# Softmax sums of the first tile: two pairs through VectorE transposes instead of TensorE, with another order of work in front of the first matmuls

## The chip, the cores and the metric

The kernel runs on one core of one Trainium2 chip. The metric is device time in microseconds, from the program's start to its end. Before the change it is 294.37 us, the median of three runs (294.26 to 294.83); the profiled execution has a span of 293.0 us. Times inside the text are microseconds from the start of that span unless they are called durations.

## The reference

Two stages are computed one after the other. The first is attention within chunks of 64 rows, for 8 batches and 8 heads of 64; the second is a feed-forward block with an exact GELU on the 4608 tokens that come out.

```python
# attention: q, k, v are [8, 8, 576, 64]; chunks of 64 rows
scores = (1/8) * q_c @ k_c.T                      # 64 x 64 per chunk and head
attn = exp(scores - max) ; attn = attn / sum(attn)
x = (attn @ v_c)  ->  [4608, 512]                 # heads side by side
# feed-forward
h = x @ w_in                                      # [4608, 2048]
g = 0.5 * h * (1 + erf(h / sqrt(2)))
out = g @ w_out                                   # [4608, 512], fp32
```

The kernel leaves the maximum out (the scores are small) and divides by the sum at the end: it multiplies `attn @ v` by the reciprocal of the sum of the exponentials.

## The kernel before

The tokens are taken in nine tiles of 512 (`MT`), numbered t = 0 to 8. Heads are taken as four pairs g = 0 to 3 (`G`), so that a pair fills 128 partitions. For every tile the attention gives `x`, [128, 4, 512]: one pair per K slice of the first matmul. Then mm1 makes 16 blocks of `h` (four matmuls of 128x512 each, one per K slice) and mm2 makes the output from them. While TensorE runs mm1 and mm2 of tile t, the attention of tile t+1 is fitted in between. Only tile 0 has nothing to hide behind: its attention, and the casts of the first weights, run before the first matmul of mm1.

The program gives the order of instructions itself: on each engine they run in the order in which the program issues them.

The attention of tile 0, one pair at a time, is: `T` (transposes of q and k on TensorE, and copies from PSUM), `S` (scores on TensorE, exp on ScalarE into `pT`), the sum, and `A` (attn @ v on TensorE, times the reciprocal on VectorE).

```python
    def att_Tk(t, g, copies):                       # k of a pair: two halves, two copies
        tp = transposed(t, "k", g)
        for r in range(2):
            sl = slice(CH * r, CH * (r + 1))
            copies[r](k_bds[g][sl, :, sl]..., tp[sl])

    def att_sum(t, g, later=False):                 # sums by VectorE
        pT = tiles[t]["pT", g]
        sum_ps = ps_at.tile([P, MT], f32, tag="at", name="sum_ps")
        nc.tensor.matmul(sum_ps[:], ones_bd[:], pT[:], start=True, stop=True)
        ...
        nc.vector.transpose(t1[:], sum_ps[:].rearrange("p (n e) -> p n e", e=32))
        def rest_of_it():
            nc.vector.reciprocal(r1[:], t1[:, :, 0])
            nc.vector.transpose(rc[:], r1[:].to_broadcast([P, NB, 32]))
        ...

    def att_sum_pe(t, g):                           # sums and their spreading by TensorE
        pT = tiles[t]["pT", g]
        sT = ps_at.tile([P, MT // P, 2], f32, tag="at", name="sT")
        for m in range(MT // P):
            nc.tensor.matmul(sT[:, m], pT[...][:, m * P:(m + 1) * P], ones_r[:], start=True, stop=True)
        rr = work.tile([P, MT // P, 2], f32, tag="rr", name="rr", bufs=2)
        nc.vector.reciprocal(rr[:], sT[:])

        def spread():
            pool, tag = (ps_mm, "mm") if g < 2 else (ps_tp, "tp")
            rc_ps = pool.tile([P, NB, 32], f32, tag=tag, name="rc_ps")
            flat = rc_ps[:].rearrange("p n e -> p (n e)")
            for m in range(MT // P):
                for r in (1, 0):
                    nc.tensor.transpose(flat[0:CH * (r + 1), m * P:(m + 1) * P],
                                        rr[:, m, r:r + 1].to_broadcast([P, CH * (r + 1)]), ident_f[:])
            rc = work.tile([P, NB, 32], f32, tag="rc", name="rc", bufs=4)
            nc.scalar.copy(rc[:], rc_ps[:])
            tiles[t]["rc", g] = rc
        return spread

    def att_av(t, g):
        av_ps = ps_at.tile(...)
        for i in range(CT):
            nc.tensor.matmul(av_ps[:, i, :], v_bds[t % NV][:, i, g, :], st["pT", g][:, i, :], ...)
        nc.vector.tensor_tensor(x, av, rc, op=mybir.AluOpType.mult)
    ...
    def mm1_slot(t, f, n=1, between={}):            # tile 0 begins with n = 2: f0 and f1 slice by slice
        for ks in range(KS):
            for a in range(n):
                nc.tensor.matmul(h_ps[a][:], w_in_sb[:, ks, (f + a) * P:...], st["x"][:, ks, :], ...)
```

The start of the program, in its order (cut from the scores of pair 0 on):

```python
        S_[0]()
        T[3]()
        cast_qk(0, "q", 2, DV)
        keep_warm(1)
        T[4]()
        keep_warm(1)
        S_[1]()
        cast_qk(0, "q", 3, DV)
        p0 = att_sum_pe(0, 0)
        T[5]()
        p0()
        T[6]()
        T[7]()
        p1 = att_sum_pe(0, 1)
        S_[2]()
        p1()
        keep_warm(1)
        S_[3]()
        p2 = att_sum_pe(0, 2)
        p2()
        A[0]()
        A[1]()
        p3 = att_sum_pe(0, 3)
        p3()
        A[2]()
        A[3]()
        win.append(load_w_in(NWC - 1))
        wout = [load_w_out(0)]
        act_table(Act.Gelu)
        for i, eng in enumerate((PO, DV, DV, PO)):
            win[0](i, eng)                          # casts of w_in block f = i
        ... # then the casts of the other w_in chunks, by DV and PO in turn,
            # with two memsets of v_bd on PO between them
        phase(0, ...)                               # mm1 and mm2 of tile 0
```

`DV`, `AC` and `PO` are a copy or cast on VectorE, ScalarE and GpSimd. `keep_warm(n)` runs n matmuls on zeros, whose result nobody reads. `w_in` comes in four chunks of four blocks: chunks 0 and 1 in two DMAs each (blocks 0-1 and 2-3), chunks 2 and 3 in one.

Of the kernel before, what the change touches and what calls it, by code (L numbers as in the profile page):

```python
# [11 lines left out]
def kernel(  # L12
# [9 lines left out]
    nc = tc.nc  # L22
    P = 128
    f32 = mybir.dt.float32
# [4 lines left out]
    CH = 64  # L29
    NC = S // CH  # L30
    J = 4
# [115 lines left out]
    def att_Tq(t, g, copy):  # L147
        tp = transposed(t, "q", g)
        qT = work.tile([P, CT, CH], bf16, tag="qT", name="qT", bufs=5)
        copy(qT[:].rearrange("p i (c j) -> p i c j", j=J), tp)  # L150
        tiles[t]["qT", g] = qT

    def att_Tk(t, g, copies):
        tp = transposed(t, "k", g)
        for r in range(2):
            sl = slice(CH * r, CH * (r + 1))
            copies[r](k_bds[g][sl, :, sl].rearrange("p i (c j) -> p i c j", j=J), tp[sl])  # L157


    def flip(t, nm):  # L160
# [101 lines left out]
    def att_sum_pe(t, g):  # L262
# [4 lines that stand above are left out]
            nc.tensor.matmul(sT[:, m], pT[:].rearrange("p i c -> p (i c)")[:, m * P:(m + 1) * P], ones_r[:],  # L267
                             start=True, stop=True)
        rr = work.tile([P, MT // P, 2], f32, tag="rr", name="rr", bufs=2)
        nc.vector.reciprocal(rr[:], sT[:])  # L270

        def spread():


            pool, tag = (ps_mm, "mm") if g < 2 else (ps_tp, "tp")
            rc_ps = pool.tile([P, NB, 32], f32, tag=tag, name="rc_ps")
            flat = rc_ps[:].rearrange("p n e -> p (n e)")
            for m in range(MT // P):
                for r in (1, 0):
                    nc.tensor.transpose(flat[0:CH * (r + 1), m * P:(m + 1) * P],  # L280
                                        rr[:, m, r:r + 1].to_broadcast([P, CH * (r + 1)]), ident_f[:])
            rc = work.tile([P, NB, 32], f32, tag="rc", name="rc", bufs=4)
            nc.scalar.copy(rc[:], rc_ps[:])
            tiles[t]["rc", g] = rc
        return spread

# [17 lines left out]
    def att_units(t, cq=DV, ck=DV):  # L304
        tiles[t]["x"] = xpool.tile([P, G, MT], bf16, tag="x", name="x")
        T = []
        for g in range(G):
            T += [lambda g=g: att_Tq(t, g, cq), lambda g=g: att_Tk(t, g, (AC, DV) if t == 0 and g > 1 else [AC if t == 0 or g < 2 else DV] * 2)]
        S_ = [lambda g=g: att_S(t, g) for g in range(G)]
        if t > 1:  # L310
            T = [lambda g=g: flip_k(t, g, ck) for g in range(G)]
            S_ = [lambda g=g: (att_S_flipped(t, g), att_part(t, g)) for g in range(G)]
        if t > 0:
            U = [lambda g=g: att_total(t, g, g + 2) for g in (0, 2)] + [lambda g=g: att_rc(t, g) for g in range(G)]
        else:
            U = [lambda g=g: att_sum(t, g) for g in range(G)]
        A = [lambda g=g: att_av(t, g) for g in range(G)]
        return T, S_, U, A
# [111 lines left out]
    def load_w_out(c):  # L430
        raw = stage_tile()[:].rearrange("p (f n) -> p f n", f=FC)
        nc.sync.dma_start(raw, w_out_v[:, c * FC:(c + 1) * FC, :])

        def cast(i, copy):
            copy(w_out_sb[:, c * FC + i, :], raw[:, i, :])
        return cast
# [13 lines left out]
    def act_table(func):  # L450
        nc.scalar.activation(act_scratch[:], rest[:, 0:1], func)  # L451

    with tc.manual_schedule():
        for g in range(G):
            for nm in "qk":
                load_qk(0, nm, 2 * g, 2 * g + 2)
        load_v(0)
        win = [load_w_in(c, 2 if c < 2 else 1) for c in range(NWC - 1)]
        act_table(Act.Exp)
        keep_warm(7)  # L460
        zero_k(k_bds[0], nc.gpsimd)
        zero_k(k_bds[1], nc.gpsimd)
        zero_v(0, nc.vector)
        T, S_, U, A = att_units(0, DV, AC)
        cast_qk(0, "k", 0, PO)
        zero_k(k_bds[2], nc.gpsimd)
        cast_qk(0, "k", 1, PO)
        zero_k(k_bds[3], nc.gpsimd)
        cast_qk(0, "k", 2, PO)
        cast_qk(0, "k", 3, PO)  # L470
        for g in range(G):
            cast_v(0, 0, PO, slice(g, g + 1))
            cast_v(0, 1, PO, slice(g, g + 1))
        cast_qk(0, "q", 0, DV)
        T[0]()
        cast_qk(0, "q", 1, DV)
        T[1]()
        keep_warm(3)
        T[2]()
# [5 lines that stand above are left out]
        keep_warm(1)  # L485
        S_[1]()
        cast_qk(0, "q", 3, DV)
        p0 = att_sum_pe(0, 0)
        T[5]()
        p0()  # L490
        T[6]()
        T[7]()
        p1 = att_sum_pe(0, 1)
        S_[2]()
        p1()
        keep_warm(1)
        S_[3]()
        p2 = att_sum_pe(0, 2)
        p2()
        A[0]()  # L500
        A[1]()
        p3 = att_sum_pe(0, 3)
        p3()
        A[2]()
        A[3]()
        win.append(load_w_in(NWC - 1))
        wout = [load_w_out(0)]
        act_table(Act.Gelu)
        for i, eng in enumerate((PO, DV, DV, PO)):
            win[0](i, eng)  # L510
        load_qk(1, "q")
        wout.append(load_w_out(1))
        for c in range(1, NWC):
            for i in range(4):
                win[c](i, DV if i % 2 == 0 else PO)
            if c == 1:
                load_qk(1, "k")
            else:
                wout.append(load_w_out(c))
            if c < 3:  # L520
                r = slice(CH * (c - 1), CH * c)
                o = slice(CH * (2 - c), CH * (3 - c))
                nc.gpsimd.memset(v_bds[1][r, :, :, o], 0.0)
        for i in range(FC):
            wout[0](i, DV if i % 2 == 0 else PO)
        load_v(1)
        for g in range(G):
            cast_qk(1, "q", g, DV if g == 0 else PO)
        for i in range(FC):
            wout[1](i, DV if i % 2 == 0 else PO)  # L530
        for g in range(G):
            cast_qk(1, "k", g, DV if g % 2 == 0 else PO)
        for i in range(FC):
            wout[2](i, PO)
        for i in range(2):
            wout[3](i, PO)
        for g in range(G):
            for r in range(2):
                cast_v(1, r, PO, slice(g, g + 1))

        T, S_, U, A = att_units(1, AC, AC)
        def next_qk():
            for nm in "qk":
                load_qk(2, nm)
        over = []

        def sums():
            over.append(att_sums(1))
            over[0](1)
        phase(0, {}, {0: [lambda: act_table(Act.Exp)],  # L550
                      2: [T[0]], 3: [T[2]], 4: [T[4], T[6]], 7: [T[1], T[3]], 8: [T[5], S_[0]],
                      9: [T[7], S_[1], next_qk], 10: [S_[2], lambda: att_sum(1, 0), lambda: wout[3](2, DV)],
                      11: [lambda: wout[3](3, AC), S_[3]], 12: [sums],
                      13: [A[0], lambda: over[0](2), lambda: over[0](3), U[3]], 14: [A[1], U[4]], 15: [A[2], U[5]]},
              by_rows=True)
        last_av = {1: [A[3], lambda: rows_out(0, 3)]}
        pool_cast_qk(2)
        for t in range(1, NT):
            nxt = t + 1 < NT
            if nxt:  # L560
                T, S_, U, A = att_units(t + 1)
                for nm in "qk":
                    flip(t + 1, nm)
                if t == 1:
                    load_v(2)
                for r in range(2):
                    cast_v(t + 1, r, PO)
                if t + 2 < NT:
                    load_all(t + 2)
                    pool_cast_qk(t + 2)  # L570
            e1, e2 = {}, {}
            if nxt:
                e1 = {8: [T[0]], 10: [T[1]], 12: [T[2]], 14: [T[3]]}
                e2 = {0: [lambda: act_table(Act.Exp), S_[0]], 1: [S_[1]], 2: [S_[2]],
                      3: [S_[3], U[0]], 5: [U[1], lambda: act_table(Act.Gelu)],
                      7: [U[2], A[0]], 8: [U[3], A[1]], 10: [U[4], A[2]], 12: [U[5], A[3]]}
            phase(t, e1, e2, between=last_av if t == 1 else {})
# [28 lines left out]
```

The softmax here doesn't subtract the row's maximum and nothing guards it: scores larger than these inputs give would overflow.

## Time and profile before

| engine | busy us | share of the span |
|---|---|---|
| PE (TensorE matmul) | 281.5 | 96% |
| DVE (VectorE) | 155.0 | 53% |
| ACT (ScalarE) | 169.5 | 58% |
| POOL (GpSimd) | 98.7 | 34% |

The profile is one execution, recorded by the hardware. TensorE is busy nearly throughout, so the places where it is not are what is looked at; they lie in the first 22 us. A view of busy time by stretches gives TensorE 3.33 us of the 5 from 10 to 15, 3.51 of the 5 from 15 to 20, and 3.66 of the 5 from 20 to 25; from 57 to 100 it is busy all 43. The granted clock is 1.00 in every stretch. The share of the DMA engines is 1.06 of their capacity, as the view counts it, from 15 to 30, so data is arriving as fast as it can while the attention of tile 0 is worked out.

In a line of the timeline the columns are: start, duration, engine, line of the kernel, operation, tile written `<-` tiles read, shape, count, and in brackets how long the engine had been idle before and what ended that. In the chain of waits a line is a piece of the chain that ended last: start, duration, and what it was.

### The profile page before, as it was taken

Reading aid. Unit: us, or ns where it says so; the run is one execution under the profiler, and the core shown is the slowest. Engines: PE = TensorE matmul, PEld = TensorE weight load, DVE = VectorE, ACT = ScalarE, POOL = GpSimd, SP = SyncE. Lnnn points to the kernel's source line nnn. Section 1 sums busy time; section 2 is a strip of 40 time slices with the busy share of each in tenths; the row PEclk is TensorE's granted clock in tenths of the full one; section 3 lists DMA queues with packets and bytes.
Section 4 is the critical chain, followed back from the end, with each engine's and each line's share of the span. In section 5 each row is a group of like instructions: output and inputs, shape, how many; then the busy total and the mean of one; then the engine's idle time right before and its main releaser. Section 6 shows DMA issues by size and latency. Waiting matters only on the chain.

```text
span 293.0 us, 4901 instructions
## 1 busy us (share of the span) xinstructions
PE 281.5 (96%) x1874; PEld 140.6 (48%) x1874; DVE 155.0 (53%) x264; ACT 169.5 (58%) x328; POOL 98.7 (34%) x136
## 2 busy tenths in 40 slices
PE   7669999999999999999999999999999999999994
PEld 2554455445544554455445444554455445544443
DVE  5649317744842794449525964496168515850011
ACT  3546756978536853685268627862786268726400
POOL 6759758605650850075005600650003520000000
PEclk9999999999999999999999999999999999999999
DMA  6899998899859913991399339922999990020032
GB/s 213 218 359 404 396 340 230 276 217 284 215 185 296 247 73 97 283 267 64 99 217 298 95 100 275 267 69 103 192 127 125 235 186 2 36 106 4 0 72 72
DMA packets 96887, 53.79 MB, mean 184 GB/s; under 512 B 68576, under 2 KB 89312, under 8 KB 96864
## 3 DMA queue, kind: packets, MB, share of 16 engines
q1 hardware_dynamic: 96704, 53.36, 68.8%
q8 instruction: 14, 0.23, 0.3%
q10 hardware_dynamic: 160, 0.13, 0.2%
q14 instruction: 9, 0.07, 0.1%
HBM read 36.70 MB, written 9.44 MB: 157 GB/s over the span
## 4 chain that ended last, share of the span: by engine, by line
PE 90%; DVE 3%; DMA 2%; ACT 1%; SPq 1%; issue 1%; DVEq 0%
PE h_ps L331 42%; PE y_ps L347 37%; PE y_ps L387 3%; PE av_ps L292 2%; DMA arrival<-in_q_dram 2%; PE s_ps L180 2%; PE rc_ps L280 1%; DVE x L299 1%; PE y_ps L372 1%; SPq L112 1%; DVE rc L259 1%; PE tp L144 1%; ACT k_bd L157 1%; PE s_ps L192 0%; ACT rb L229 0%
## 5 line engine op out<-in xcount | busy, mean ns | idle before, releaser
L331 PE MATMUL h_ps<-x,w_in_sb 128*128 128x512 bf16 x576 | 126.3, 379 | 1.5 <-DVE w_in_sb L427 1.3
L334 ACT ACTIVATE h<-h_ps 128x512 bf16<-128x512 f32 x144 | 85.5, 597 | 63.6 <-PE h_ps L331 63.5
L347 PE MATMUL y_ps<-w_out_sb,h 128*128 128x512 bf16 x512 | 120.5, 379 | 0.0
L331 PEld LDWEIGHTS <-w_in_sb 128*128 128x128 bf16 x576 | 56.2, 98 | 69.3 <-DVE w_in_sb L427 1.6
L347 PEld LDWEIGHTS <-h 128*128 128x128 bf16 x512 | 46.0, 98 | 46.5 <-issue 0.2
L172 DVE COPY k_bd<-k_t 64x512 bf16<-64x512 bf16 x56 | 35.2, 629 | 50.4 <-DMA k_t<-k_nat 49.4
L133 POOL CAST q_nat<-arrival 128x512 bf16<-128x512 f32 x31 | 20.9, 711 | 96.2 <-DMA arrival<-in_q_dram 96.2
L137 POOL CAST v_bd<-arrival 64x512 bf16<-64x512 f32 (+1 forms) x30 | 36.4, 1212 | 20.1 <-DMA arrival<-in_v_dram 13.1
L299 DVE TENSOR_TENSOR x<-av_ps,rc 128x512 bf16<-128x512 f32 x36 | 24.7, 691 | 6.5 <-PE av_ps L292 2.9
L133 POOL CAST k_nat<-arrival 128x512 bf16<-128x512 f32 x34 | 20.1, 626 | 13.6 <-DMA arrival<-in_k_dram 13.5
L239 DVE STREAM_TRANSPOSE pt<-pT 128x256 f32<-128x256 f32 x28 | 12.2, 437 | 22.9 <-ACT pT L183 22.9
L451 ACT ACT_TABLE_LOAD x18 | 23.1, 1283 | 1.1 <-PEq L590 0.7
L356 DVE COPY y_sb<-y_ps 128x512 f32<-128x512 f32 x11 | 7.6, 689 | 29.2 <-PE y_ps L347 29.2
L356 ACT COPY y_sb<-y_ps 128x512 f32<-128x512 f32 x24 | 13.8, 580 | 14.7 <-PE y_ps L347 14.4
L259 DVE STREAM_TRANSPOSE rc<-rb 128x512 f32<-128x512 f32 x31 | 21.4, 692 | 0.2 <-ACT rb L229 0.2
L242 DVE TENSOR_REDUCE part<-pt 128x16 f32<-128x512 bf16 x28 | 19.2, 686 | 1.0
L250 ACT COPY other<-part 32x32 f32<-32x32 f32 x56 | 12.1, 215 | 10.4 <-DVE part L242 9.9
L292 PEld LDWEIGHTS <-v_bd 128*128 128x128 bf16 x288 | 13.0, 98 | 7.6
L183 ACT ACTIVATE pT<-s_ps 128x512 bf16<-128x512 f32 x28 | 14.7, 590 | 0.0
L292 PE MATMUL av_ps<-pT,v_bd 128*128 128x64 bf16 x288 | 13.9, 193 | 0.0
L180 PEld LDWEIGHTS <-k_bd 128*128 128x128 bf16 x224 | 10.4, 98 | 6.6
L387 PE MATMUL y_ps<-w_out_sb,h 128*128 128x512 bf16 x48 | 12.0, 379 | 0.3 <-ACT h L334 0.3
(67 smaller groups left out, 141.2 us busy)
## 6 DMA issues: line engine op xcount, KB each, us to landing
arrival<-in_v_dram SPq DMA_DIRECT2D x72, 128.0 KB, 4.1
out_dram<-y_sb SPq DMA_DIRECT2D x32, 256.0 KB, 2.1
arrival<-in_q_dram SPq DMA_DIRECT2D x7, 1024.0 KB, 6.2
arrival<-in_k_dram SPq DMA_DIRECT2D x7, 1024.0 KB, 9.1
arrival<-in_moe_w_out_dram SPq DMA_DIRECT2D x4, 1024.0 KB, 12.5
arrival<-in_moe_w_in_dram SPq DMA_DIRECT2D x4, 512.0 KB, 6.0
arrival<-in_moe_w_in_dram SPq DMA_DIRECT2D x2, 1024.0 KB, 9.5
arrival<-in_q_dram SPq DMA_DIRECT2D x4, 256.0 KB, 5.4
```

Of the source, the lines that this page charges most:

```text
L133: copy(st[nm][:, g].rearrange("p j r d -> p r j d"), st[nm + "f"][:, 2 * g:2 * g + 2])
L137: copy(v_bds[t % NV][sl, :, gs, sl].rearrange("p i g d -> p g i d"), tiles[t]["vf"][sl, gs])
L172: copy(k_bds[g][sl, :, sl].rearrange("p i (c j) -> p i c j", j=J), src[sl])
L259: nc.vector.transpose(rc[:], src.to_broadcast([P, NB, 32]))
L292: nc.tensor.matmul(av_ps[:, i, :], v_bds[t % NV][:, i, g, :], st["pT", g][:, i, :], start=True, stop=True)
L299: nc.vector.tensor_tensor(x, av, rc, op=mybir.AluOpType.mult)
L331: nc.tensor.matmul(h_ps[a][:], w_in_sb[:, ks, (f + a) * P:(f + a + 1) * P], st["x"][:, ks, :], start=(ks == 0), stop=(ks == KS - 1))
L334: nc.scalar.activation(st["h"][:, f + a, :], h_ps[a][:], Act.Gelu)
L347: nc.tensor.matmul(y_ps[:], st["h"][:, f, ms * P:(ms + 1) * P], w_out_sb[:, f, :], start=(f == 0), stop=(f == FF - 1))
L356: (AC if ms < 3 and t + 1 < NT else DV)(y_sb[:], y_ps[:])
L387: nc.tensor.matmul(tiles[t]["y_ps", ms][:], tiles[t]["h"][:, f, ms * P:(ms + 1) * P], w_out_sb[:, f, :], start=(f == 0), stop=False)
L451: nc.scalar.activation(act_scratch[:], rest[:, 0:1], func)
```

## The change

The sums of pairs 0 and 1 of tile 0 go from the TensorE form (`att_sum_pe`) back to the VectorE form (`att_sum`); pairs 2 and 3 keep the TensorE form, whose spreading now always uses the `ps_mm` buffers. Both halves of every k copy of tile 0 are ScalarE's (VectorE had one half of pairs 2 and 3). The sums of pairs 2 and 3 are both made ahead of the first attn @ v, and the spreadings go between A[0], A[1] and A[2]. Two `keep_warm(1)` are added. One of the two VectorE casts of w_in chunk 0 goes to ScalarE, ahead of the table load for GELU. The purpose is to have `x` and the first weight blocks ready sooner, by another share of work between the engines and another order.

```diff
-    def att_Tk(t, g, copies):
+    def att_Tk(t, g, copy):
         tp = transposed(t, "k", g)
         for r in range(2):
             sl = slice(CH * r, CH * (r + 1))
-            copies[r](k_bds[g][sl, :, sl].rearrange("p i (c j) -> p i c j", j=J), tp[sl])
+            copy(k_bds[g][sl, :, sl].rearrange("p i (c j) -> p i c j", j=J), tp[sl])
@@ att_sum_pe
         def spread():
-            pool, tag = (ps_mm, "mm") if g < 2 else (ps_tp, "tp")
-            rc_ps = pool.tile([P, NB, 32], f32, tag=tag, name="rc_ps")
-            flat = rc_ps[:].rearrange("p n e -> p (n e)")
+            rc_ps = ps_mm.tile([P, MT], f32, tag="mm", name="rc_ps")
@@ att_units
-            T += [lambda g=g: att_Tq(t, g, cq), lambda g=g: att_Tk(t, g, (AC, DV) if t == 0 and g > 1 else [AC if t == 0 or g < 2 else DV] * 2)]
+            T += [lambda g=g: att_Tq(t, g, cq), lambda g=g: att_Tk(t, g, ck if t == 0 or g < 2 else DV)]
@@ the start of the program
         S_[1]()
         cast_qk(0, "q", 3, DV)
-        p0 = att_sum_pe(0, 0)
+        U[0]()                      # att_sum(0, 0)
         T[5]()
-        p0()
         T[6]()
         T[7]()
-        p1 = att_sum_pe(0, 1)
+        U[1]()                      # att_sum(0, 1)
         S_[2]()
-        p1()
         keep_warm(1)
         S_[3]()
+        keep_warm(1)
         p2 = att_sum_pe(0, 2)
+        p3 = att_sum_pe(0, 3)
+        A[0]()
         p2()
-        A[0]()
         A[1]()
-        p3 = att_sum_pe(0, 3)
         p3()
         A[2]()
+        keep_warm(1)
         A[3]()
         win.append(load_w_in(NWC - 1))
         wout = [load_w_out(0)]
+        for i, eng in enumerate((PO, AC, DV, PO)):
+            win[0](i, eng)
         act_table(Act.Gelu)
-        for i, eng in enumerate((PO, DV, DV, PO)):
-            win[0](i, eng)
```

(The comments at `U[0]` and `U[1]` are added here. The rest of the diff rewrites the same expressions without `flat`.)

More of the change, by code (lines that the diff above doesn't have):

```diff
@@ L272, in spread @@
         def spread():
-            pool, tag = (ps_mm, "mm") if g < 2 else (ps_tp, "tp")
-            rc_ps = pool.tile([P, NB, 32], f32, tag=tag, name="rc_ps")
-            flat = rc_ps[:].rearrange("p n e -> p (n e)")
+            rc_ps = ps_mm.tile([P, MT], f32, tag="mm", name="rc_ps")
             for m in range(MT // P):
                 for r in (1, 0):
-                    nc.tensor.transpose(flat[0:CH * (r + 1), m * P:(m + 1) * P],
+                    nc.tensor.transpose(rc_ps[0:CH * (r + 1), m * P:(m + 1) * P],
                                         rr[:, m, r:r + 1].to_broadcast([P, CH * (r + 1)]), ident_f[:])
             rc = work.tile([P, NB, 32], f32, tag="rc", name="rc", bufs=4)
-            nc.scalar.copy(rc[:], rc_ps[:])
+            nc.scalar.copy(rc[:].rearrange("p n e -> p (n e)"), rc_ps[:])
             tiles[t]["rc", g] = rc
```

## The prediction

> **What bounds the kernel now.** I read the waits of TensorE first, then the chain of waits of the first 24 us, then the timeline of the stretch where the two meet. The waits of TensorE from 15 us to the end:
>
> ```profile
> PE rc_ps L280 <- DVE rr L270: 1.5, 2, 1.2
> PE h_ps L331 <- DVE w_in_sb L427: 1.3, 1, 1.3
> PE y_ps L387 <- ACT h L334: 0.3, 1, 0.3
> PE tp L144 <- ACT k_bd L157: 0.2, 1, 0.2
> ```
>
> The columns are: who waited for whom, us in total, times, longest. The first two lie ahead of 22.1 us; the last two, 0.5 us together, are all that is left in the 271 us after it. So from 22.1 us on the kernel is TensorE's work laid end to end, and the time is 22.1 plus that. The question is only when the stream of mm1 starts. The chain of waits up to there:
>
> ```profile
> 16.18 1.09 PE rc_ps L280 x8
> 17.27 0.25 PE av_ps L292 x8
> 17.52 0.02 issue
> 17.54 0.26 DVE x L299
> ...
> 18.15 0.68 DVE x L299
> 18.83 0.13 DVE rr L270
> 18.95 0.04 issue
> 19.00 1.09 PE rc_ps L280 x8
> 20.09 0.25 PE av_ps L292 x8
> ...
> 21.03 0.68 DVE x L299
> 21.71 0.34 DVE w_in_sb L427
> 22.06 0.05 issue
> 22.11 1.90 PE h_ps L331 x8
> ```
>
> VectorE and TensorE hand work to and fro. The reciprocal of pair 3 stands behind the two x of pairs 0 and 1 on VectorE (18.83); only then can its spreading run (19.00), then A[2] and A[3], then their x, and after those the cast of weight block f=1, for which the second matmul of mm1 waits. And what the weights themselves allow, from the timeline:
>
> ```profile
> 17.82 0.61 POOL L427 CAST w_in_sb<-arrival 128x512 bf16<-128x512 f32 x1 [0.60 <-DMA arrival<-in_moe_w_in_dram]
> 19.09 0.61 POOL L427 CAST w_in_sb<-arrival 128x512 bf16<-128x512 f32 x1 [0.65 <-DMA arrival<-in_moe_w_in_dram]
> 20.76 0.61 POOL L427 CAST w_in_sb<-arrival 128x512 bf16<-128x512 f32 x1 [1.06 <-DMA arrival<-in_moe_w_in_dram]
> 22.08 0.78 POOL L427 CAST w_in_sb<-arrival 128x512 bf16<-128x512 f32 x1 [0.70 <-DMA arrival<-in_moe_w_in_dram]
> ```
>
> GpSimd stood ready each time, so these are the arrivals: blocks 0-1 at 17.8, 2-3 at 19.1, 4-5 at 20.75, 6-7 at 22.05. Chunk 2 (blocks 8-11) was issued near 15.9 and took 8.7, so it lands near 24.6; chunk 3 lands at 27.1, where VectorE waited for it. mm1 cannot start before 17.8 + 0.61 = 18.4. It really starts at 22.11: up to 3.7 us are there to be had.
>
> **What the Trainium skill says.** "SBUF — State Buffer", section "Who interferes with whom": VectorE casts in a two-port mode and GpSimd share one pair of ports as an exclusive lock, held for a whole instruction. The trace agrees: VectorE casts of w_in take 416 ns at the least, 824 in the median, and one 2098, beside GpSimd's memset of 22.80 to 24.87. "ScalarE: Activation LUTs", section "What ACT_TABLE_LOAD costs", gives 1283 ns for the load; the trace has 1.28 at 20.73. "TensorE: Matmul & The Clock Gate", Part 1, says that an idle window of about 3.4 us halves the clock. The trace shows four transposes taking 0.60 us together at 4.50 and 0.40 at 7.51, and no slow form after that, with idle stretches of up to 1.3 us.
>
> **The change, part by part.** I follow the new order on each engine from the point up to which both kernels are the same (S[1] at 10.14, q cast of pair 3 on VectorE to 10.89), with durations from this trace.
>
> *VectorE's sums of pairs 0 and 1.* From tile 1, where this form already runs: transpose 0.72, reciprocal 0.25, transpose 0.71, together 1.74 from start to end. They take from TensorE two times (4 matmuls of `sT`, about 0.1 of issue, and 8 transposes of `rc_ps`, 1.09 or 0.9 of issue) and give it two 128x512 matmuls of 0.22 issue: TensorE is freed of about 1.6 us. ScalarE loses two copies of 0.58 and gets two k halves of 0.58: nothing. VectorE loses two halves of 0.69 and two reciprocals of 0.2 (1.8), and gets 2 x 1.74 = 3.5: 1.7 more, in a stretch where it had gaps.
>
> *VectorE:* sum matmul of pair 0 ends at 10.75, so rc0 is 10.85 to 12.5; qT of pair 3 12.5 to 13.2; rc1 13.2 to 14.85; rr2 and rr3 to 15.2.
>
> *ScalarE:* exp of pair 1 to 11.2, k of pair 2 to 12.2, k of pair 3 (its GpSimd cast ends at 11.98 as now, the transposes at 12.4) to 13.55; exp of pair 2 to 14.1; S[3] can run at 13.6, so exp of pair 3 to 14.65. Now that exp runs from 15.87 to 16.47: 1.8 us sooner.
>
> *TensorE:* sT2 and sT3 by 14.95, A[0] 14.9 to 15.2, spreading of pair 2 15.1 to 16.2 (rr2 is there, as it is no longer behind any x), A[1] to 16.4, spreading of pair 3 16.3 to 17.4, A[2] to 17.55, keep_warm, A[3] at 17.7 to 18.05. Its v halves come from GpSimd's casts, 11.93 to 17.22 as now: in time. ScalarE's copies of the two spreadings end at 16.8 and 18.0.
>
> *x:* pair 0 at 15.9, pair 1 at 17.1, pair 2 at 18.25, pair 3 at 18.9.
>
> *Weights:* block 0 by GpSimd 18.43; block 1 by ScalarE, after its copy, 18.0 to 18.6 (0.61, as its cast of w_out); the GELU table then 18.6 to 20.05; block 2 by VectorE 19.1 to 19.9; block 3 by GpSimd 19.7.
>
> *mm1:* f0 and f1 alternate over the slices from 18.5, eight matmuls of 0.216 (12.26 us for 56, less the 0.16 of the last one's tail), so f1 starts at 18.65 and both end at 20.2; x of pair 3 is wanted at 19.5. Now the second matmul starts at 22.11 and seven end at 23.6. The stream from f2 on starts 3.4 us sooner.
>
> *Given back to arrivals.* At 0.865 us a block from 20.2, f4 is wanted at 21.9 (arrives 20.75, cast 0.43 to 0.8), f6 at 23.65 (22.05), f8 at 25.35, f12 at 28.8 (27.1; GpSimd's memset to 28.4 may hold the port, then the cast). Block 8 lands at 24.6, but the memset holds the port to about 25, and a cast is 0.43 to 0.8: ready at 25.4 to 25.9. That and f12 cost about 0.45. Net: 3.4 - 0.45 = about 3.0.
>
> *Later:* is anything fixed by DMA within 3 us of its use? w_out blocks 8-11 are cast from 40.64 to 42.93 and block 8 is used at 45.16; v of tile 1 is cast 45.74 to 51.19 and used by A at 51.05 to 54.99 (a pair each 1.36, wanted each 1.1: 0.4 of slack remains for pair 2); k of tile 2 is copied 62.44 to 67.4 and used from 68.7 to 72.0; v of tile 2 is cast by 71.73 and used at 75.66. All keep between 0.4 and 2 us after a shift of 3, and thereafter the tiles repeat with TensorE as the bound. So the shift should reach the end: 294.4 - 3.0 = 291.4.
>
> **The rivals.** (1) *The chain moves to VectorE.* Its 1.7 us more could delay qT of pair 3, rr2 and rr3, and so x of pair 3. For: on VectorE everything is in order, and rc1 is needed by nobody before 16.4 but stands ahead of rr2. Against: x of pair 3 has 0.6 us of slack, and S[3] waits for ScalarE's k copy (13.55) rather than qT (13.2). If every step came 1 us later, about 0.4 of the gain would go: 291.8. (2) *The weights become the bound.* mm1 follows the arrivals closely from 19 to 29. If VectorE's cast of block 6 fell behind the memset (its sibling took 2.1), f6 would wait until 25.1, 1.5 us: 292.5. (3) *Nothing is gained, as later arrivals hold tile 1 or 2.* Speaking for it, the DMA engines are at their limit to 40 us. Then 293 to 294. The slacks just listed speak against. (4) *The clock halves*, since TensorE has less to do from 11 to 15 us; a slow stretch to 18.5 would cost 1 to 2 us, 292.5 to 293.5. Its longest gap there would be 0.7 us, and keep_warm was put in; unlikely. (5) *All goes right and stalls are nil*: 291.0.
>
> **Range and chances.** Most weight is on 291.0 to 291.8, with a tail upward from (2) to (4) and little below 290.8, because 18.4 is the floor set by the arrival of block 0, 3.7 us ahead of 22.1. The range is 290.7 to 292.7. Two per cent are 5.9 us, more than the whole idle time that the change can reach; a loss of that size would need a wait that no view shows. Faster by over 2%: 0.02; within: 0.96; slower: 0.02.
>
> **What would show it.** In the profile of the changed kernel: exp of pair 3 near 14.1; x of pair 3 ending near 18.9; the stream of mm1 from 18.5 with the wait for w_in on VectorE gone; small waits of TensorE for w_in casts between 23 and 29; no wait over 0.5 us after 35; the last mm2 three us sooner. Wrong would be: the stream not starting before 20, or its start sooner and the end not, with a wait for a DMA or a cast in tiles 0 to 2.

## The result, and the profile after

The changed kernel takes 291.5 us (median of four runs, 291.02 to 291.77) against 294.56 us of the kernel before in the same session: ratio 0.9895, 95% interval 0.9877 to 0.9912, or 3.1 us less. The span of the profiled execution falls from 293.0 to 290.0 us.

The waits of TensorE from 15 us to the end, in the changed kernel (who waited for whom, us in total, times, longest):

```profile
PE h_ps L327 <- DVE w_in_sb L423: 0.9, 2, 0.7
PE h_ps L327 <- POOL w_in_sb L423: 0.4, 1, 0.4
```

The wait of the spreading for the reciprocal (`rc_ps <- rr`, 1.5) is gone. What is left of the front is waiting for weight blocks: 0.4 ahead of the first matmul of mm1, 0.9 inside mm1. Two more waits, of 0.3 and 0.2, are those of before. Where these waits lie, in the timeline of the changed kernel:

```profile
13.06 1.09 ACT L194 ACTIVATE pT<-s_ps 128x512 bf16<-128x512 f32 x2
...
14.31 0.39 DVE L270 RECIPROCAL rr<-sT 128x8 f32<-128x8 f32 x2
...
17.10 1.29 DVE L295 TENSOR_TENSOR x<-av_ps,rc 128x512 bf16<-128x512 f32 x2 [0.52 <-PE av_ps L288]
17.17 0.61 POOL L423 CAST w_in_sb<-arrival 128x512 bf16<-128x512 f32 x1 [0.70 <-DMA arrival<-in_moe_w_in_dram]
...
17.84 3.63 PE L327 MATMUL h_ps<-x,w_in_sb 128*128 128x512 bf16 x16 [0.40 <-POOL w_in_sb L423]
...
21.68 0.43 DVE L423 CAST w_in_sb<-arrival 128x512 bf16<-128x512 f32 x1 [2.83 <-DMA arrival<-in_moe_w_in_dram]
...
22.17 3.63 PE L327 MATMUL h_ps<-x,w_in_sb 128*128 128x512 bf16 x16 [0.71 <-DVE w_in_sb L423]
```

The exp of pair 3 in the kernel before:

```profile
15.87 0.60 ACT L194 ACTIVATE pT<-s_ps 128x512 bf16<-128x512 f32 x1
```

Both exps end at 14.15 (pair 3's at 16.47 before), both reciprocals are made one after the other at 14.31, and x of pairs 2 and 3 is ready at 18.39 instead of 21.72. Some 0.4 us of that are not the change's: the scores of pair 1, up to which both kernels do the same work, already ran at 9.74 in this execution, against 10.14 in the profile of the kernel before. The stream of mm1 starts at 17.84, right at the end of GpSimd's cast of block 0, which itself began on the block's arrival. After blocks 0 to 3 TensorE waits 0.71 us for block 4: VectorE had been idle 2.83 us, so that is arrival too. The chain of waits of the changed kernel, from 14 to 26 us, says the same: where before it went to and fro between VectorE and TensorE, it is now one transfer, that of chunk 2, ended by a cast and the matmul of block 8:

```profile
14.62 10.85 DMA arrival<-in_moe_w_in_dram
...
25.49 0.44 DVE w_in_sb L423
...
25.98 0.39 PE h_ps L327
```

mm2 of tile 0 starts at 32.89 in place of 35.71. That difference, 2.8 us, is the same at the last mm2 (272.32 against 275.13): nothing is lost or won in 240 us in between.

### The profile page after: what moved, and what is told of

The parts are those of the page before. It is cut to its first block, busy times and chain, and to the rows that moved or that the text cites. A ratio compares the mean times of both kernels' runs of the same rounds, so it can differ in the third digit from the quotient of the medians.

```text
span 290.0 us, 4861 instructions
## 1 busy us (share of the span) xinstructions
PE 280.2 (97%) x1854; PEld 138.3 (48%) x1854; DVE 151.2 (52%) x265; ACT 170.3 (59%) x329; POOL 97.6 (34%) x136
## 4 chain that ended last, share of the span: by engine, by line
PE 87%; DMA 5%; SPq 3%; DVE 2%; ACT 1%; issue 0%; DVEq 0%
PE h_ps L327 40%; PE y_ps L343 37%; DMA arrival<-in_moe_w_in_dram 4%; PE y_ps L383 3%; PE av_ps L288 2%; PE s_ps L180 2%; SPq L129 2%; DMA arrival<-in_q_dram 2%; PE y_ps L368 1%; SPq L420 1%; DVE x L295 1%; DVE rc L259 1%; PE tp L144 1%; ACT k_bd L157 0%; PE s_ps L192 0%
## 5 line engine op out<-in xcount | busy, mean ns | idle before, releaser
L133 POOL CAST q_nat<-arrival 128x512 bf16<-128x512 f32 x31 | 19.2, 659 | 91.7 <-DMA arrival<-in_q_dram 66.8
```

Of the source, the lines that this page charges most:

```text
L133: copy(st[nm][:, g].rearrange("p j r d -> p r j d"), st[nm + "f"][:, 2 * g:2 * g + 2])
```

## The experiments

Eleven kernels and the changed kernel again, each beside runs of the kernel before on the same chip. Ratios are to the kernel before, with 95% intervals; a time without a reference is the run's median.

### One piece at a time, in the kernel before

**Order alone.**

```diff
         p2 = att_sum_pe(0, 2)
+        p3 = att_sum_pe(0, 3)
+        A[0]()
         p2()
-        A[0]()
         A[1]()
-        p3 = att_sum_pe(0, 3)
         p3()
         A[2]()
```

> The kernel before with one thing of the change alone: the order of the sums and spreadings of pairs 2 and 3 (sums of both, A[0], spreading 2, A[1], spreading 3, A[2]). All four sums stay on TensorE. Theory (readiness: the time is set by when x of pair 3 and weight block 1 are ready): the reciprocal of pair 3 no longer stands behind two x on VectorE, x of pair 3 ends near 20.7 in place of 21.7, and the time falls by about 1.0 us, ratio 0.9965. Rival (work: what counts is that TensorE is freed of the two fp32 spreadings): no TensorE work is taken away here, so 0, ratio 1.000.

Measured: 0.9953 (0.9935 to 0.9972), 1.3 us less. The rival's 1.000 is excluded. The timeline of this kernel:

```profile
20.37 13.77 PE L331 MATMUL h_ps<-x,w_in_sb 128*128 128x512 bf16 x63 [1.34 <-DVE w_in_sb L427]
```

The wait of 1.34 us for VectorE's cast is exactly that of before; it has only moved forward, from 22.11 to 20.37. About 0.7 of these 1.7 us belong to this execution's earlier arrival of k (the reciprocal of pair 2, ahead of which nothing was changed, starts at 15.19 against 15.92); the remaining 1.0 is what was expected.

**Cast alone.**

```diff
-        act_table(Act.Gelu)
-        for i, eng in enumerate((PO, DV, DV, PO)):
+        for i, eng in enumerate((PO, AC, DV, PO)):
             win[0](i, eng)
+        act_table(Act.Gelu)
```

> The kernel before with another thing alone: the cast of w_in block 1 on ScalarE, ahead of the GELU table load, in place of VectorE. Theory (readiness): the second matmul of mm1 no longer waits for VectorE's cast behind x of pair 3; it starts at 21.3 in place of 22.1, and the time falls by about 0.7 us, ratio 0.9975. Rival (work on TensorE): 0, ratio 1.000.

Measured: 0.9950 (0.9933 to 0.9968), 1.5 us less, twice the expected 0.7, whose ratio of 0.9975 lies outside the interval. The wait of 1.34 us for VectorE's cast has become one of 0.51 for ScalarE's:

```profile
20.12 13.77 PE L331 MATMUL h_ps<-x,w_in_sb 128*128 128x512 bf16 x63 [0.51 <-ACT w_in_sb L427]
```

The difference of the two waits, 0.83, is near the expectation. The rest of the measured 1.5 is left open; the profiled execution again had its k earlier, by 1.2 us.

**Order and cast together.** Both edits above.

> The two edits before together: order and ScalarE cast, all sums on TensorE. Theory (readiness): the two add up, as the second only shortens what follows the first: 1.7 us, ratio 0.994; then the sums on VectorE and the k copies are left with 1.3 us of the 3.1. Rival (work on TensorE): at most 0.3 us, ratio 0.999 or more, and the sums would carry nearly all.

Measured: 0.9909 (0.9890 to 0.9927), 2.7 us less: the two add up (1.3 + 1.5), and they bring more than the theory's 1.7 (its 0.994 lies outside the interval). No work is taken from TensorE here, all four sums are still its own, and most of the changed kernel's gain is there. So the rival that puts nearly all of the gain down to the two spreadings taken off TensorE falls.

The traces say the same with the arrivals taken out. Up to the reciprocal of pair 2 these four kernels do the same work, so the time from there to the start of mm2 of tile 0 shows the edits alone. Its two ends, before and with order and cast:

```profile
15.92 0.21 DVE L270 RECIPROCAL rr<-sT 128x8 f32<-128x8 f32 x1 [1.71 <-PE sT L267]
35.71 0.59 PE L387 MATMUL y_ps<-w_out_sb,h 128*128 128x512 bf16 x2
```
```profile
14.97 0.21 DVE L270 RECIPROCAL rr<-sT 128x8 f32<-128x8 f32 x1 [1.71 <-PE sT L267]
32.94 0.59 PE L387 MATMUL y_ps<-w_out_sb,h 128*128 128x512 bf16 x2
```

That is 19.79 us before, 18.79 with the order alone, 18.97 with the cast alone and 17.97 with both: 1.00, 0.82 and 1.82 less. The medians of the runs gave 0.3 to 0.9 more than that; why is not shown.

### One piece taken back, in the changed kernel

The changed kernel was run again beside the next three, for a measure on the same chip.

> The changed kernel again, unaltered, as the measure for the three beside it: 291.5, ratio to before 0.9895.

Measured: 290.92 us, 0.9886 (0.9867 to 0.9906). This execution shows what the first did not:

```profile
17.74 0.61 POOL L423 CAST w_in_sb<-arrival 128x512 bf16<-128x512 f32 x1 [1.49 <-DMA arrival<-in_moe_w_in_dram]
...
20.34 0.43 DVE L423 CAST w_in_sb<-arrival 128x512 bf16<-128x512 f32 x1 [0.92 <-DMA arrival<-in_moe_w_in_dram]
```
```profile
18.40 13.99 PE L327 MATMUL h_ps<-x,w_in_sb 128*128 128x512 bf16 x63 [1.15 <-POOL w_in_sb L423]
```

Here GpSimd's cast of block 0, which starts on the arrival, began 0.57 us later than in the first profile, and the first cast of blocks 4-5 1.34 us earlier (20.34 against 21.68). TensorE waited 1.15 us ahead of the stream and not at all inside it. The place of the wait is another in this execution; that it is an arrival is the same in both.

**Cast of block 1 back on VectorE.** `(PO, AC, DV, PO)` becomes `(PO, DV, DV, PO)`.

> The changed kernel with the cast of w_in block 1 back on VectorE, behind the four x. Theory (the arrival of blocks 4 to 7 fixes when mm1 of tile 0 gets on, whatever its start): the start of the stream is 0.8 us later, but TensorE's 0.7 us of waiting for block 4 takes that up, and the time is 0 to 0.2 us above the changed kernel. Rival (each step of the start counts in full): 0.8 us above it, ratio to before 0.992.

Measured: 0.9921 (0.9897 to 0.9946), 291.56 us, 0.64 above the run beside it by the medians and 1.0 by the ratios. That is nearer the rival's 0.8 than the theory's 0 to 0.2, though the intervals overlap. In the profiled execution the second matmul, and with it the stream, starts at 18.57, only 0.17 later than in the run beside it, as block 0 was there early this time (16.87):

```profile
18.57 13.77 PE L327 MATMUL h_ps<-x,w_in_sb 128*128 128x512 bf16 x62 [0.64 <-DVE w_in_sb L423]
```

What I had assumed, that a wait of 0.7 us at block 4 stands ready to take up a late start, is not so in every execution: in this one, as in the repeated run, there is none. mm2 of tile 0 starts at 32.18 here and at 32.23 in the run beside it, so this pair of profiles does not show where the 0.64 us of the medians lie.

**Sums of pairs 0 and 1 back on TensorE.**

```diff
-        U[0]()
+        p0 = att_sum_pe(0, 0)
         T[5]()
+        p0()
         T[6]()
         T[7]()
-        U[1]()
+        p1 = att_sum_pe(0, 1)
         S_[2]()
+        p1()
```

> The changed kernel with the sums of pairs 0 and 1 back on TensorE and their spreadings on TensorE and ScalarE; k copies, order, cast and keep_warm as changed. Theory (arrival): the two ScalarE copies of the spreadings stand ahead of the exp of pairs 2 and 3 and make x of pair 3 about 1.2 us later; the wait for block 4 takes up 0.7 of it: 0.2 to 0.6 us above the changed kernel. Rival (TensorE's 1.6 us of work more count in full): 1.6 us above it, ratio to before 0.995.

Measured: 0.9918 (0.9902 to 0.9935), 291.7 us, 0.8 above the run beside it by the medians and 0.9 by the ratios. The rival's 1.6 (0.995) is excluded; 0.8 is a little over the theory's 0.2 to 0.6. x of pair 3 is 0.76 later (17.67 + 1.29, against 16.91 + 1.29 in the run beside it), and TensorE waits for ScalarE once ahead of the spreadings and once at the cast of block 1:

```profile
PE sT L267 <- ACT pT L194: 0.6, 1, 0.6
PE h_ps L327 <- DVE x L295: 0.5, 1, 0.5
PE h_ps L327 <- ACT w_in_sb L423: 0.5, 1, 0.5
```

The middle line lies in tile 1, at 53.9. But block 0 arrived late in both executions (17.86 and 17.74), and mm2 of tile 0 starts only 0.12 us later than in the run beside it (32.35 against 32.23); the profiled time is longer mainly by the wait in tile 1. That the sums on VectorE are worth some 0.8 us is what the runs say; by which wait is not shown.

This kernel differs from order and cast together in the k copies, the buffers of the spreading and the added keep_warm alone, and the two measure the same, on different chips: 291.70 and 291.71 us (0.9918 and 0.9909). So these pieces together show no effect beyond the noise.

**Order of before, in the changed kernel.** The first diff above, reversed.

> The changed kernel with the order of before for pairs 2 and 3 (sum 2, spreading 2, A[0], A[1], sum 3, spreading 3, A[2]); sums of pairs 0 and 1 on VectorE, k copies and cast stay as changed. Theory (readiness): the reciprocal of pair 3 is again behind two x, its spreading starts near 17.3, ScalarE's cast of block 1 stands behind the copy of that spreading and ends near 19.7, and the time is 0.8 to 1.3 us above the changed kernel, ratio to before 0.992 to 0.994. Rival (the VectorE sums had made enough room that the order no longer matters, as arrivals set the start): at most 0.3 us, ratio 0.989 to 0.990.

Measured: 0.9913 (0.9885 to 0.9942), 292.18 us; by the ratios 0.5 to 0.8 us above the changed kernel, which had 0.9895 and 0.9886. The mechanism is the expected one,

```profile
15.92 1.29 DVE L295 TENSOR_TENSOR x<-av_ps,rc 128x512 bf16<-128x512 f32 x2 [1.41 <-PE av_ps L288]
17.13 0.20 DVE L270 RECIPROCAL rr<-sT 128x8 f32<-128x8 f32 x1
17.38 0.82 PEld L276 LDWEIGHTS rc_ps<-ident_f,rr 128*128 128x128 f32 x8 [1.27 <-DVE rr L270]
```

the reciprocal of pair 3 behind the two x, and the stream from 19.66 (expected: near 19.7), but the size is at or below the low end of the theory's 0.8 to 1.3. The interval holds the theory's 0.992 to 0.994 and the rival's 0.989 to 0.990, so the size alone does not decide. The traces show both at work. This execution and the first profile of the changed kernel reach the end of both exps together (14.18 and 14.15). From there the old order makes the stream of mm1 some 1.6 us later (19.66 from the second matmul on, against 17.84 from the first), so the order does still matter; but mm2 of tile 0 starts only 0.4 us later (33.27 against 32.89), as the later stream does not have to wait inside mm1.

So the order, the cast and the sums each cost some 0.5 to 1.0 us when taken back alone, with intervals about as wide as these differences, so that none of the three is measured well. In the kernel before, order and cast gave 1.3 and 1.5. That a step is worth less where waits for arrivals stand next to it is seen for the order, in the last pair of profiles; for the cast it is argued.

### Is it the arrival of the weights?

**mm1 of tile 0 from blocks 0 to 3 only.** It leaves out the waiting for blocks 4 to 15.

```diff
-                nc.tensor.matmul(h_ps[a][:], w_in_sb[:, ks, (f + a) * P:(f + a + 1) * P], ...
+                # wb(b) = b % 4 in tile 0, else b
+                nc.tensor.matmul(h_ps[a][:], w_in_sb[:, ks, wb(f + a) * P:(wb(f + a) + 1) * P], ...
```

> The changed kernel, in which mm1 of tile 0 uses weight blocks 0 to 3 four times over instead of blocks 0 to 15 (so tile 0's output is not the reference's): it leaves out nothing but the waiting for the later blocks' arrival and cast. Theory (after the change the arrivals of w_in are the bound of mm1 in tile 0): the waits of TensorE for w_in casts after 18 us, 0.9 us in the profile, vanish, and the time is 0.9 us below that of the changed kernel, 290.6, ratio to before 0.9865. Rival (what is won there is lost to later arrivals, w_out, q, k and v of tile 1): the time stays at 291.5, with new waits of TensorE between 30 and 57 us.

Measured: 0.9903 (0.9878 to 0.9927). The profiled execution did what the theory says: one unbroken stream of 64 from 18.06, mm2 at 31.88, no new wait later. But the median is 291.35 us, within the changed kernel's 290.92 and 291.50, and the theory's 0.9865 lies outside the interval. The 0.9 us inside mm1 were those of one execution and not the kernel's typical loss; as theory of the typical run, this one fell. The profiled run, 290.83 us, is one of the two fastest of six: what the others lost, and whether to later arrivals as the rival has it, no trace shows.

**mm1 of tile 0 from a resident block of zeros.** It leaves out the waiting for all of w_in, block 0 too.

```diff
+                # tile 0: rest[:, 0:P] in place of w_in_sb[...]
```

> The changed kernel, in which all of mm1 of tile 0 takes its weights from a block of zeros that lies in SBUF from the start (tile 0's output is not the reference's). It leaves out the whole waiting for w_in in tile 0, of the first block too; all loads and casts stay. Theory (the start of the stream is set by the arrival of block 0 plus its cast): the stream starts right behind A[3], near 17.3, in place of 17.8 to 18.4, and the time falls by 0.7 to 1.2 us below the changed kernel, ratio to before 0.985 to 0.987. Rival (x or ScalarE's GELU is the bound, or later arrivals take it back): no change, ratio 0.989.

Measured: 0.9884 (0.9854 to 0.9915), 291.38 us: no change that can be seen, as the rival says, though the wide interval holds the theory's 0.987 too. Its profile shows a taking back:

```profile
17.19 14.06 PE L327 MATMUL h_ps<-x,rest 128*128 128x512 bf16 x63
```
```profile
41.35 1.02 PE L383 MATMUL y_ps<-w_out_sb,h 128*128 128x512 bf16 x4 [0.54 <-POOL w_out_sb L431]
...
47.63 0.41 PE L288 MATMUL av_ps<-pT,v_bd 128*128 128x64 bf16 x8 [0.16 <-POOL v_bd L137]
```

Freed of w_in, the stream starts behind A[3] at 17.19 and mm2 of tile 0 at 31.09, 1.1 us ahead of the repeated run's 32.23. But then TensorE waits for w_out block 8 (41.35) and for v of tile 1 (47.63), and from the start of mm2 of tile 0 to the start of mm1 of tile 1 it takes 20.33 us (31.09 to 51.42); in the kernel before and in the changed kernel these are 18.63 and 18.67. 1.7 us go where 1.1 had been won, and some 0.3 of them come back later. GpSimd's casts of w_out from block 8 on, which wait for an arrival, begin at the same time in this kernel and in the one with four blocks, although mm2 of tile 0 starts 0.8 us sooner here:

```profile
40.69 2.29 POOL L431 CAST w_out_sb<-arrival 128x512 bf16<-128x512 f32 x4 [0.99 <-DMA arrival<-in_moe_w_out_dram]
```
```profile
40.77 2.29 POOL L432 CAST w_out_sb<-arrival 128x512 bf16<-128x512 f32 x4 [0.93 <-DMA arrival<-in_moe_w_out_dram]
```

With four blocks, block 8 is used at 41.44, about when its cast is done; here it is used at 41.35, and the 0.8 us are gone. Below, for every profiled execution, the start of mm2 of tile 0, and what remains from there to the end of the run (its device time less that start):

| kernel | mm2 of tile 0 starts | from there to the end |
|---|---|---|
| before | 35.71 | 259.1 |
| order alone | 33.98 | 259.1 |
| cast alone | 33.73 | 258.8 |
| order of before, in the changed kernel | 33.27 | 258.8 |
| block 0 ahead of v (below) | 32.97 | 258.8 |
| order and cast | 32.94 | 258.8 |
| changed | 32.89 | 258.9 |
| sums taken back | 32.35 | 259.3 |
| changed, again | 32.23 | 258.8 |
| cast taken back | 32.18 | 259.1 |
| without keep_warm (below) | 32.16 | 259.9 |
| smaller pieces (below) | 32.02 | 259.8 |
| four blocks | 31.88 | 259.0 |
| resident zeros | 31.09 | 260.3 |

In eleven executions what remains is 258.8 to 259.3 us. In the other three it is 259.8 to 260.3, and these are the three in which TensorE waits 0.5 to 0.6 us for w_out block 8: with resident zeros because TensorE is early, in the other two because the block is ready later (GpSimd's casts begin at 41.61 and 41.90). These are single executions; the medians do not resolve it.

### Two attempts to do better, and the keep_warm

**w_in in smaller pieces.** Chunks 0 and 1 in four DMAs, chunk 2 in two: `load_w_in(c, 4 if c < 2 else 2)`.

> The changed kernel with w_in loaded in smaller pieces: chunks 0 and 1 in four DMAs each (a block each), chunk 2 in two, in place of 2, 2 and 1. The bytes and their order are the same. Theory (arrival): block 0 lands 0.6 us and block 4 about 0.65 us sooner, as they no longer wait for their neighbours; the waits of TensorE for w_in, 0.9 us after the start, shrink to 0.3 or less, and the time falls by 0.4 to 0.7 us below the changed kernel. Rival (the issue of seven more DMAs, some 0.5 us each on the queue, delays all that follows): no gain, or up to 1 us above it.

Measured: 0.9941 (0.9917 to 0.9964), 1.5 us slower than the changed kernel beside it. The rival holds in its direction; the loss is above its 1 us, although the DMAs are five more and not seven (11 in place of 6). The queue's timeline:

```profile
12.21 8.72 SPq L420 DMA_DIRECT2D arrival<-in_moe_w_in_dram  x11
21.04 0.64 SPq L428 DMA_DIRECT2D arrival<-in_moe_w_out_dram  x1
```

In the changed kernel run beside it the six loads of w_in took the queue from 11.92 to 17.80, and the first of w_out went out at 17.90; here it is 21.04. mm2 starts at 32.02, early, but from there to the end it takes 259.8, with 0.6 us of waiting for w_out. The profiled run, 291.82 us, is 0.6 below this kernel's median, so what the slower ones lost is not seen.

**Block 0 ahead of v of pair 3.**

```diff
-        load_v(0)                                   # then w_in
+        load_v(0, range(G - 1))                     # then blocks 0-1, v of pair 3, the rest of w_in
...
-        keep_warm(1)
-        A[3]()
+        mm1_slot(0, 0, 2, {3: [A[3]]})              # A[3] ahead of K slice 3
```

> The changed kernel with blocks 0 and 1 of w_in loaded ahead of v of pair 3, GpSimd's cast of block 0 ahead of its casts of that v, and A[3] moved into mm1, ahead of K slice 3 of blocks 0 and 1, the only place where x of pair 3 is wanted; one keep_warm goes. Theory (arrival of block 0): it lands about 1.4 us sooner, the first matmul starts at 16.8 in place of 17.8 to 18.4, TensorE then waits some 0.7 us at A[3] and x of pair 3, and the time falls by 0.3 to 0.6 us, ratio to before 0.987. Rival (v of pair 3 and its GpSimd casts, 1.3 us, become the bound): no gain, or up to 1 us lost.

Measured: 0.9905 (0.9879 to 0.9931): no gain, and the theory's 0.987 lies outside the interval. The block came early (cast at 15.44) and the first matmul ran at 16.91, as expected; but block 1 still waited for ScalarE, whose cast stands behind its copy of the last spreading, and A[3], put behind six matmuls that waited, gave x of pair 3 only at 20.3:

```profile
18.03 1.25 PE L327 MATMUL h_ps<-x,w_in_sb 128*128 128x512 bf16 x4 [0.74 <-ACT w_in_sb L426]
...
20.37 12.76 PE L327 MATMUL h_ps<-x,w_in_sb 128*128 128x512 bf16 x57 [0.85 <-DVE x L295]
```

GpSimd's casts of v of pair 3 had ended at 17.27, 1.85 us before A[3]: it was not v that became the bound, as the rival had it, but my own order.

**Without keep_warm.** The two added ones and the one behind S[2] are taken out.

> The changed kernel without its two added keep_warm matmuls and without the one behind the scores of pair 2, so that TensorE has three gaps of 0.5 to 1 us between 12 and 17.5 us. Rival of the prediction (the clock halves when TensorE has less to do): [...]matmuls of 128x512 at twice their duration there, and 1 to 2 us more than the changed kernel. Theory (readiness): nobody reads their result and nothing waits behind them, so the same time, ratio to before 0.989, and no slow matmul.

Measured: 0.9919 (0.9895 to 0.9942), 292.23 us; the theory's 0.989 lies just outside the interval. There is no slow matmul: the eight score matmuls take 0.41 us behind a gap of 0.81, the eight transposes of a spreading 1.07, as in the changed kernel, and mm2 starts at 32.16. The halved clock is not seen:

```profile
13.61 0.41 PE L192 MATMUL s_ps<-qT,k_bd 128*128 128x64 bf16 x8 [0.81 <-ACT k_bd L157]
```

In this execution k of tile 1 landed late (GpSimd waited 2.59 us for it), and TensorE waited 0.55 us for w_out; from mm2 to the end it took 259.9. Whether the 0.8 us above the changed kernel are keep_warm's or this lateness's is not settled.

## Why the prediction was right

The predicted time, 291.4, is 0.1 from the measured one, and the gain, 3.0, from 3.1. That closeness is partly luck: the repeated measurement gave 290.92 and 3.3, and steps that were off in the single executions offset one another. What was right is the mechanism. By its own steps:

- *The chain to 22.11 is what is to be shortened.* Right, and shown: two edits that touch only this chain, and take no work off TensorE, bring 2.7 us.
- *The reciprocals ahead of every x.* Right: rr at 14.31, and taking the order back restores the wait of 1.2 us.
- *Sums of pairs 0 and 1 on VectorE.* The runs give them some 0.8 us when they alone are taken back, but the gain beyond order and cast is only 0.4, within the noise, and no profile shows the wait that they shorten.
- *VectorE has room for 1.7 us more.* Right, just: VectorE is busy 4.67 of the 5 us from 10 to 15, and the reciprocals follow rc1 without a gap. Its load did not become the bound (first rival), as the spreading of pair 2 starts at 14.55 right behind A[0]; x of pairs 2 and 3 came at 18.39, 0.5 ahead of the predicted 18.9, of which 0.4 is the earlier start of this execution. The slack of x of pair 3 was larger than stated: eight matmuls of 0.216 from 18.5 want it at 19.8 and not at 19.5.
- *mm1 from 18.5.* The first profile has 17.84, the second 18.40. The step's rule, cast of block 0 on arrival, held in both; taking one execution's arrivals for fixed times did not.
- *Given back to arrivals: 0.45 at blocks 8 and 12.* Neither size nor place held in a single execution. Measured were 0.71 at block 4 and 0.18 at block 8 in one, and none inside mm1 in the other; 0.45 lies between. GpSimd's memset holding VectorE off, of which I made part of it, mattered little: block 8 waited for its arrival at 25.49.
- *The weights become the bound* (second rival). Half right: they set the start in both profiles, but in the repeated run nothing inside mm1.
- *A shift of 3 us reaches the end.* Right, and close to where it stops being so: in the profile with resident zeros one more microsecond is taken back by w_out and v of tile 1 (third rival).
- *The clock* (fourth rival). No slow matmul from 7 us on, with or without the three keep_warm.

## What to carry to other kernels

On an engine that works in order, look for the small instruction that everyone waits for (a reciprocal of 0.2 us) and for what stands ahead of it; moving it ahead of two long ones brought 1.3 us here, with no work taken off any engine. Gains at the front of a kernel can end where the next transfer is due, so list for each transfer when it lands and when it is wanted, and take the list from more than one execution. Splitting loads to have the first piece sooner can delay what stands behind them on the same queue: here the first load of w_out went out 3.1 us later.

## What the runs showed that was not expected

- Arrivals scatter between executions although the first loads are the same: GpSimd's cast of k of pair 3, which starts on its arrival, began between 10.03 and 11.37 us over the profiles. The kernel before was profiled in the latest of them, so part of any shift between two single profiles is this.
- Blocks 4-5 landed 1.3 us behind blocks 2-3 in one execution of the changed kernel and 3.2 us in the other; the later pieces then followed at nearly the same distances (1.3 to 1.4, then 2.5 to 2.6 us) in both. Why one gap is long is not known.
- A VectorE cast of w_in beside GpSimd's took 0.43 us (21.68), and GpSimd's, started 0.03 later, 0.87 in place of 0.61. That the one which starts second pays agrees with the Trainium skill ("SBUF — State Buffer", section "Who interferes with whom"), by which whoever issues first has the shared ports for its whole instruction and the other waits. Waiting out the remaining 0.40 in full would have made 1.01, so the measured delay is smaller than that.
